# Last expert's row tiles one after the other with two scatters inside the branch, and the first gate's short tile scattered first

## The chip, the core and the metric

The program runs on one core of one Trainium2 chip. The metric is the device time of one execution in microseconds (us). Engines are named as in the profile: PE (matrix engine), PEld (its weight loads), DVE, ACT, POOL (GpSimd) and SP; a q behind a name (POOLq, SPq) is the engine's sequencer, which decodes, waits and branches while the engine itself may be idle or still busy. L1971 is line 1971 of the kernel before.

## What is computed

Attention with a decay over 4 batches of 576 tokens and 8 heads of 64 gives 2304 tokens of 512 numbers. A first mixture of 8 experts (512 to 1024 to 512, ReLU) sends each token to its best expert. A second mixture does the same with a hard capacity of 288 tokens per expert, assigned greedily by the largest logits. Cut to what matters here:

```python
def _moe_ref(x, w_gate, w_output_gate, w1, w2):
    logits = x @ w_gate
    e_idx = np.argmax(logits, axis=1)
    ...
        out[mask] = gate_w[mask, None] * eom[mask, e, None] * (np.maximum(x[mask] @ w1[e], 0.0) @ w2[e])
def _moe2_ref(x, w_gate, w1, w2):
    cap = N // E                       # 288
    ...                                # the largest logits take the places
    for e in range(E):
        mask = assigned == e
        out[mask] = np.maximum(x[mask] @ w1[e], 0.0) @ w2[e]
```

## The kernel before

The work goes through three stages on the same engines. Attention runs over 16 pairs of heads; `Router.gate` (L375 to L458) follows each batch: it makes logits, ranks each token inside its expert, and writes the rows of x to the DRAM array `xs` in expert order with five indirect scatters on POOL (L452), one for each 128-token tile. The fifth tile of a batch has only 64 real tokens, in partitions 64 to 127; the other 64 partitions get an index out of bounds (L442) and are dropped. After the fourth gate, `Moe1` fetches `xs` expert by expert, and its first weights and rows wait for the landing of the last scatter.

The second mixture is `Moe2Quick`. An expert has 288 rows: two tiles of 128 and a rest of 32. W1 runs column-wise for all 288 (L732). W2 runs by rows in `by_row` (L789): for each of 8 slices f of the hidden layer, three matmuls of 512 columns for tile 0 and three for tile 1 (L796), and the rest in two blocks of 16 small matmuls, `over(0)` after f = 3 and `over(4)` before f = 7 (L803). The three results are copied by ACT (L817 for the rest, L827 for the tiles) and scattered to the output on POOL (`send`, L1971). Each PE matmul of the tiles is one third of an fp32 product; an expert's W2 weights are all split (ACT L698, POOL L702) before its `by_row` ends.

For the first seven experts the scatters run during the next expert. The eighth writes to tiles `last` and `lastr`, which live outside the branch, and `finish` (L1977) scatters them at the very end of the program. Between the two lies control flow that every engine goes through:

```python
    with tc.If(uneven < 1):            # L2072, the normal case: both mixtures
        ...
            quick.go(redo, last)
    with tc.If(uneven > 0):            # L2080, not taken
        ...
    again = nc.values_load(redo[0:1, 0:1], min_val=0, max_val=1)    # L2088
    with tc.If(again > 0):             # L2089, not taken
        ...
    late["quick"].finish(tc, *last, out)
```

An engine that skips a body still does two things at its end: it waits until its own work and, on POOL, all DMAs that POOL has issued (DMASW0 to DMASW7, eight semaphores) have come in, and then it brings the semaphores to the values that the body would have left. On POOL that last step is INC_SWDGE_SEM. The order of instructions on each engine is the order in which the generators yield them; there is no scheduler that would move them.

Of the kernel before, what the change touches and what calls it, by code (L numbers as in the profile page):

```python
# [17 lines left out]
B, H, S, D = 4, 8, 576, 64  # L18
N = B * S
DM = H * D  # L20
E = 8
NP = H // 2
NQ = 4
SQ = NQ * 128
TL = S - SQ
# [289 lines left out]
class Router:  # L315
# [59 lines left out]
    def gate(self, b, ots, x, r):  # L375
        nc, p, ps = self.nc, self.p, self.att.ps_t
        us = p.tile([128, S], F32, name="us")
        for c0 in (0, S // 2):
# [4 lines left out]
            nc.scalar.copy(us[:, c0:c0 + S // 2], t[:, :S // 2])  # L383
# [48 lines left out]
        nc.scalar.activation(los, los, AF.Exp, scale=-1.0)  # L432
        pos = p.tile([128, NI, E], F32, name="pos")
        nc.vector.tensor_add(pos, po[:, :NI, :], ec(self.carry))
        nc.vector.tensor_add(self.carry, self.carry, po[:, NI, :])
        yield
        nc.vector.tensor_mul(pos, pos, ohb)
        sl = p.tile([128, NI], F32, name="sl")
        nc.vector.tensor_reduce(sl, pos, axis=AX.X, op=ALU.add)
        idx = p.tile([128, NI], I32, name="idx")  # L440
        nc.vector.tensor_copy(idx, sl)
        nc.vector.memset(idx[:T0, NQ:], E * RS)  # L442
        yield
        sm = p.tile([128, NI], F32, name="smx")
        nc.vector.tensor_reduce(sm, d, axis=AX.X, op=ALU.add)
# [4 lines left out]
        for i in range(NI):  # L450
            nc.gpsimd.memset(self.sp1, 0.0)
            st = nc.gpsimd.indirect_dma_start(  # L452
                out=self.xs[:, :], out_offset=bass.IndirectOffsetOnAxis(ap=idx[:, i:i + 1], axis=0),
                in_=x[:, i, :], in_offset=None, bounds_check=E * RS - 1, oob_is_err=False)
# [177 lines left out]
class FFN:  # L632
# [156 lines left out]
    def by_row(self, r, hs, rest, yr):  # L789
# [4 lines left out]
        if yr is None:  # L794
            yr = self.rp.tile([128, n, DM], F32, name="yr"), self.rp.tile([128, 128], F32, name="yl")
# [11 lines left out]

        for f in range(NF):
# [796 lines left out]
class Moe2Quick(Moe2):  # L1605
# [371 lines left out]
    def finish(self, tc, y, slots, out):  # L1977

        scat = []
        for t in range(3):  # L1980
            self.send(out, y, slots[:, t:t + 1], t, scat)
# [22 lines left out]
    def go(self, redo, last):  # L2004
# [12 lines left out]
        for ph in range(E):  # L2017
            self.cur = ph
            y = L.paced(f.run(ph, self.CAP, f.px if self.turning == ph else self.ready[ph][0],
                              last[0] if ph == E - 1 else None), 0.405, "gpso")  # L2020
# [12 lines left out]
def kernel(  # L2033
# [27 lines left out]
    with ExitStack() as c1:  # L2061
# [7 lines left out]
    last = ((lp.tile([128, 2, DM], F32, name="last"), lp.tile([128, 128], F32, name="lastr")),  # L2069
            lp.tile([128, 3], I32, name="slots"))  # L2070
# [9 lines left out]
    with tc.If(uneven > 0):  # L2080
# [5 lines left out]
        for t in last[0]:  # L2086
            nc.gpsimd.memset(t, 0.0)
# [49 lines left out]
```

## Time and profile before

| | |
|---|---|
| time, median of 3 runs | 764.57 us (764.44 to 764.62) |
| the profiled execution's own time | 764.5 us |
| its span in the trace | 762.8 us |
| PE busy | 689.9 us, 90% |
| POOL busy | 485.4 us, 64% |
| granted PE clock over the span | 0.957 |
| attention with its gates, to the landing of the last `xs` scatter | 0 to 222.6 us |
| second mixture's last expert, W2 by rows | 736.6 to 750.15 us |
| the last expert's three scatters on POOL | 750.9 to 754.4 us |
| end of the span | 762.8 us |

The profiled execution is 0.07 us under the median, so sums are made against 764.5 us. 1.7 us of it lie outside the span. The profile's page gives shares over the whole program; for this change only two stretches matter, the end of the last gate (205 to 223 us) and everything after 736 us, and these are read from the chain of waits, the timeline and the lists by source line, where the sequencers' own instructions show too.

### The profile page before, as it was taken

What the parts mean: (1) busy time and instruction counts of PE and PEld (TensorE: products, weight loads), DVE (VectorE), ACT (ScalarE), POOL (GpSimd) and SP (SyncE); (2) the same over time, 40 slices, a digit from 0 to 9 for tenths busy, and PEclk for the clock granted to TensorE, in tenths of its full rate; (3) what the DMA queues carried; (4) which work ended last, traced back from release to release, by engine and by line L of the source; (5) the groups of instructions that cost most, each with busy time, mean ns of one, the idle gap of its engine ahead of it and who ended that gap; (6) DMA issues with size and microseconds to landing.
All of it is one profiled execution on the core that took longest, in us unless ns stands there. A gap on an engine that the chain in (4) does not pass through costs nothing.

```text
span 762.8 us, 16050 instructions
## 1 busy us (share of the span) xinstructions
PE 689.9 (90%) x5691; PEld 571.0 (75%) x5691; DVE 367.7 (48%) x1419; ACT 382.5 (50%) x893; POOL 485.4 (64%) x504
## 2 busy tenths in 40 slices
PE   6999999999719999999999998289999999989993
PEld 3566555565419999999999998177978878888892
DVE  4776785977722132232322334756766666541020
ACT  5877776677216354555555651134535344354430
POOL 6566228172247776776776781259879778797761
PEclk9999999999959999999999999579999999999997
DMA  7588656130158362835826710348644726457201
GB/s 213 172 294 299 195 173 221 63 125 1 63 168 308 111 205 95 296 108 188 270 94 225 245 67 14 93 151 255 230 142 167 252 76 213 147 197 246 63 34 39
DMA packets 79524, 124.33 MB, mean 163 GB/s; under 512 B 11117, under 2 KB 43885, under 8 KB 79424
## 3 DMA queue, kind: packets, MB, share of 16 engines
q1 hardware_dynamic: 72944, 103.80, 41.2%
q0 software_dynamic: 6288, 18.97, 6.9%
q8 instruction: 49, 0.80, 0.5%
q14 instruction: 51, 0.42, 0.2%
q10 hardware_dynamic: 192, 0.34, 0.1%
HBM read 101.08 MB, written 22.71 MB: 162 GB/s over the span
## 4 chain that ended last, share of the span: by engine, by line
PE 54%; issue 5%; POOL 4%; DMA 3%; DVE 3%; POOLq 0%; ACT 0%; SPq 0%; DVEq 0%
PE ph L732 36%; PE ph L796 10%; POOL wl L702 3%; PE ph L803 2%; DMA xg<-x,idx 1%; PE tq L842 1%; PE sq L1783 1%; PE tq L1932 1%; PE tq L719 1%; DMA wraw<-in_moe_w_dram 1%; DMA xs<-x,idx 1%; PE tq L1036 1%; DVE cmp L1752 1%; PE gq L1892 0%; DVE xl L1939 0%
## 5 line engine op out<-in xcount | busy, mean ns | idle before, releaser
L702 POOL TENSOR_TENSOR wl<-wraw,wh 128x1024 fp32r<-128x1024 f32 x128 | 305.2, 2399 | 86.1 <-ACT wh L698 83.2
L732 PE MATMUL ph<-xh,wh 128*128 128x288 f32 (+6 forms) x512 | 160.6, 314 | 0.6 <-ACT xh L1945 0.6
L732 PE MATMUL ph<-xl,wh 128*128 128x288 f32 (+6 forms) x512 | 153.8, 300 | 1.1 <-DVE xl L1939 1.1
L698 ACT CAST wh<-wraw 128x1024 fp32r<-128x1024 f32 x128 | 132.1, 1050 | 43.7 <-DMA wraw<-in_moe_w_dram 30.6
L732 PE MATMUL ph<-xh,wl 128*128 128x288 f32 (+6 forms) x512 | 153.2, 299 | 0.0
L736 DVE SCALAR_TENSOR_TENSOR hl<-ph,hh 128x256 fp32r<-128x256 f32 (+6 forms) x128 | 56.1, 442 | 103.2 <-ACT hh L760 58.7
L174 ACT ACTIVATE z<-z,mx 128x128 f32<-128x128 f32 (+2 forms) x144 | 83.9, 583 | 36.5 <-DVE mx L177 36.0
L732 PEld LDWEIGHTS ph<-xh,wh 128*128 128x128 f32 x512 | 97.8, 191 | 4.8 <-issue 3.4
L760 ACT ACTIVATE hh<-ph 128x256 fp32r<-128x256 f32 (+6 forms) x128 | 51.4, 402 | 97.0 <-PE ph L732 93.5
L732 PEld LDWEIGHTS ph<-xl,wh 128*128 128x128 f32 x512 | 97.9, 191 | 2.1 <-DVE xl L1939 1.8
L732 PEld LDWEIGHTS ph<-xh,wl 128*128 128x128 f32 x512 | 97.6, 191 | 0.2 <-POOL wl L702 0.2
L177 DVE CUSTOM_DVE_ANT_0 z<-ps,cx 128x128 f32<-128x128 f32 (+2 forms) x144 | 68.5, 517 | 38.9 <-PE ps L188 22.5
L732 PE MATMUL ph<-hh,wh 128*128 128x288 f32 (+6 forms) x256 | 79.3, 310 | 0.0
L732 PE MATMUL ph<-hh,wl 128*128 128x288 f32 (+6 forms) x256 | 76.8, 300 | 0.9 <-POOL wl L702 0.8
L732 PE MATMUL ph<-hl,wh 128*128 128x288 f32 (+6 forms) x256 | 76.8, 300 | 0.0
L151 POOL TENSOR_SCALAR_AFFINE_SELECT cx<-cb 128x256 f32<-128x256 f32 (+1 forms) x64 | 44.3, 726 | 42.9 <-DMA cb<-c8d 19.9
L452 POOL DMA_INDIRECT xs<-x,idx x20 | 19.9, 994 | 62.0 <-DVE x L448 28.8
L796 PE MATMUL ph<-wh,hh 128*128 128x512 f32 x128 | 53.9, 421 | 0.0
L796 PE MATMUL ph<-wh,hl 128*128 128x512 f32 x128 | 50.5, 394 | 0.0
L796 PE MATMUL ph<-wl,hh 128*128 128x512 f32 x128 | 50.3, 393 | 0.0
L188 PE MATMUL ps<-kd,qd 64*128 64x128 f32 (+3 forms) x256 | 49.6, 488 | 0.1
L732 PEld LDWEIGHTS ph<-hh,wl 128*128 128x128 f32 x256 | 48.3, 189 | 1.4 <-POOL wl L702 1.4
(338 smaller groups left out, 1211.3 us busy)
## 6 DMA issues: line engine op xcount, KB each, us to landing
wraw<-in_moe_w_dram SPq DMA_DIRECT2D x128, 512.0 KB, 5.5
cb<-c8d SPq DMA_DIRECT2D x15, 576.0 KB, 6.0
xs<-zrow SPq DMA_DIRECT2D x8, 803.1 KB
xg<-xs SPq DMA_DIRECT2D x6, 771.0 KB, 9.0
kd<-in_k_dram SPq DMA_DIRECT2D x16, 288.0 KB, 6.3
qd<-in_q_dram SPq DMA_DIRECT2D x16, 288.0 KB, 3.9
vt<-in_v_dram SPq DMA_DIRECT2D x4, 1024.0 KB
x<-zrow SPq DMA_DIRECT2D x1, 1080.0 KB
```

The source lines that it names most:

```text
L151: nc.gpsimd.affine_select(cx[:, :, CB0[i]:CB0[i] + w], cb[:, :, :w], pattern=[[0, 2], [-1, w]], compare_op=ALU.is_ge, fill=-8e9, base=128 ...
L174: nc.scalar.activation(z, z, AF.Exp, bias=mx[:, c:c + 1], scale=-1.0, accum_out=sm[:, c:c + 1])
L177: nc.vector.tensor_tensor_reduce(out=z, in0=p, in1=cx, scale=-0.125, scalar=3e38, op0=ALU.add, op1=ALU.min, accum_out=mx[:, c:c + 1])
L188: nc.tensor.matmul(p[:, j, o:o + w], lhsT=qd[h, 128 * i:128 * i + 128], rhs=kd[h, :w], start=True, stop=True, skip_group_check=True)
L452: st = nc.gpsimd.indirect_dma_start(out=self.xs[:, :], out_offset=bass.IndirectOffsetOnAxis(ap=idx[:, i:i + 1], axis=0), in_=x[:, i, :], i ...
L698: nc.scalar.copy(wh, t)
L702: nc.gpsimd.tensor_sub(wl[:, q], t[:, q], wh.bitcast(F32)[:, q])
L732: mm = lambda o, w, m, st, sp: nc.tensor.matmul(o, lhsT=w, rhs=m, start=st, stop=sp)
L736: nc.vector.scalar_tensor_tensor(out=hl[:, :W], in0=p[:, :W], scalar=0.0, in1=hh.bitcast(F32)[:, :W], op0=ALU.max, op1=ALU.subtract)
L760: nc.scalar.activation(hh[:, :W], p[:, :W], AF.Relu)
L796: mm = lambda o, w, m, st, sp: nc.tensor.matmul(o, lhsT=w, rhs=m, start=st, stop=sp)
L803: nc.tensor.matmul(ps[n][32 * g:32 * g + 32, :128], lhsT=rest[f], rhs=self.raws[s][:, o:o + 128], start=f == 0, stop=f == NF - 1, skip_gro ...
```

## The change

In `by_row` the last expert gets a path of its own: `over(0)` and `over(4)` first, ACT copies the rest, POOL scatters it; then all 24 matmuls of tile 0, its copy and its scatter; then all 24 of tile 1, copied to `last`. The two scatters are issued on POOL inside the `If(uneven < 1)` body; `finish` keeps one scatter, of tile 1. In the gate the short tile gets an index tile of its own with 64 entries and is scattered first, without the dropped partitions; a sum is moved before the positions; the second half of the last gate's `us` goes through DVE and not ACT.

```diff
-            nc.scalar.copy(us[:, c0:c0 + S // 2], t[:, :S // 2])
+            self.att.evac(us[:, c0:c0 + S // 2], t[:, :S // 2], b == B - 1 and c0)
...
+        sm = p.tile([128, NI], F32, name="smx")
+        nc.vector.tensor_reduce(sm, d, axis=AX.X, op=ALU.add)
         pos = p.tile([128, NI, E], F32, name="pos")
         nc.vector.tensor_add(pos, po[:, :NI, :], ec(self.carry))
+        nc.vector.tensor_mul(pos, pos, ohb)
         nc.vector.tensor_add(self.carry, self.carry, po[:, NI, :])
         yield
-        nc.vector.tensor_mul(pos, pos, ohb)
         sl = p.tile([128, NI], F32, name="sl")
         nc.vector.tensor_reduce(sl, pos, axis=AX.X, op=ALU.add)
-        idx = p.tile([128, NI], I32, name="idx")
-        nc.vector.tensor_copy(idx, sl)
-        nc.vector.memset(idx[:T0, NQ:], E * RS)
-        yield
-        sm = p.tile([128, NI], F32, name="smx")
-        nc.vector.tensor_reduce(sm, d, axis=AX.X, op=ALU.add)
+        idt = p.tile([TL, 1], I32, name="idt")
+        nc.vector.tensor_copy(idt, sl[T0:, NQ:])
+        idx = p.tile([128, NQ], I32, name="idx")
+        nc.vector.tensor_copy(idx, sl[:, :NQ])
+        yield
...
-        for i in range(NI):
+        for ix, src in [(idt, x[T0:, NQ, :])] + [(idx[:, i:i + 1], x[:, i, :]) for i in range(NQ)]:
             nc.gpsimd.memset(self.sp1, 0.0)
             st = nc.gpsimd.indirect_dma_start(
...
+        if send:
+            for f0 in (0, 4):
+                over(f0)
+                yield 1.1
+            nc.scalar.copy(yr[1], ps[n][:, :128])
+            send(yr, 2)
+            for t in range(n):
+                w = slice(128 * t, 128 * t + 128)
+                for f in range(NF):
...
+                    mm(ps[t], hh[:, w], wh[:, m], f == 0, False)
+                    mm(ps[t], hh[:, w], wl[:, m], False, False)
+                    mm(ps[t], hl[:, w], wh[:, m], False, f == NF - 1)
+                    if f < NF - 1 or t < n - 1:
+                        yield 0.68
+                send(yr, t, ps[t])
+            return yr
...
-        scat = []
-        for t in range(3):
-            self.send(out, y, slots[:, t:t + 1], t, scat)
+        self.nc.gpsimd.indirect_dma_start(
+            out=out[:, :], out_offset=bass.IndirectOffsetOnAxis(ap=slot, axis=0), in_=y, in_offset=None,
+            bounds_check=N - 1, oob_is_err=False)
+
+    def part(self, idx, last, scat):
+
+        def send(y, t, p=None):
+            if t == 1:
+                self.nc.scalar.copy(last, p)
+                return
+            if t == 0:
+                self.nc.scalar.copy(y[0][:, 0, :], p)
+            self.nc.gpsimd.memset(self.sp1, 0.0)
+            self.send(self.o, y, idx[:, t + t // 2:t + t // 2 + 1], t, scat)
...
-        slots = last[1]
-        nc.vector.tensor_copy(slots[:, :2], idx[:, :2])
-        nc.vector.tensor_copy(slots[:, 2:], idx[:, 3:])
+        nc.vector.tensor_copy(last[1], idx[:, 1:2])
```

Three places show what moves. First POOL, from the last two weight splits (wl) to the branch that skips L2080. Before:

```order
L702 TENSOR_TENSOR wl<-wraw,wh 128x1024 [waits DMAHW0_49,PE_49,Activation_49]
L702 TENSOR_TENSOR wl<-wraw,wh 128x1024 [waits DMAHW1_49,PE_49,Activation_49]
L2072 UNCONDITIONAL_BRANCH
L2072 ISA [waits Pool_49,DMASW4_49,DMASW5_49,DMASW3_49,DMASW6_49,DMASW2_49,DMASW7_49,DMASW1_49,DMASW0_49]
L2072 UNCONDITIONAL_BRANCH
L2080 COMPARE_AND_BRANCH
```

and now, with the rest (yl) and tile 0 (yr) scattered there:

```order
L703 TENSOR_TENSOR wl<-wraw,wh 128x1024 [waits DMAHW0_49,PE_49,Activation_49]
L703 TENSOR_TENSOR wl<-wraw,wh 128x1024 [waits DMAHW1_49,PE_49,Activation_49]
L2010 MEMSET sp_433 1x1 [waits Pool_49]
L1991 DMA out_dram<-yl,idx_9509 9216x128 [waits DMASW5_49,DMASW6_49,DMASW0_49,DMASW7_49,DVE_49,Activation_49]
L2010 MEMSET sp_433 1x1 [waits Pool_49]
L1991 DMA out_dram<-yr,idx_9509 2304x512 [waits DMASW1_49,Activation_49]
L2101 UNCONDITIONAL_BRANCH
L2101 ISA [waits Pool_49,DMASW4_49,DMASW5_49,DMASW3_49,DMASW6_49,DMASW2_49,DMASW7_49,DMASW1_49,DMASW0_49]
L2101 UNCONDITIONAL_BRANCH
L2109 COMPARE_AND_BRANCH
```

Two scatters that wait for ACT now stand in POOL's queue ahead of both branches (L2080 and L2089 before, L2109 and L2117 now). Second, the end of POOL's skip of the first of these and what follows, now:

```order
L2109 ISA [waits Pool_49,Pool_sequencer_49,DMASW4_49,DMASW5_49,DMASW3_49,DMASW6_49,DMASW2_49,DMASW7_49,DMASW1_49,DMASW0_49]
L2109 UNCONDITIONAL_BRANCH
L2116 TENSOR_LOAD redo_3024 [waits DVE_49]
L2117 COMPARE_AND_BRANCH
```

These rows are the same in both kernels but for their line numbers; the ISA row waits for all eight semaphores of POOL's DMAs, and now the scatter of tile 0 is one of them. Third, DVE in the fourth gate, from the sum of the output gate's logits (los) to the scale that is written into x. The difference:

```order
 L431 TENSOR_REDUCE los<-lo_2931 128x5 [waits DVE_49]
-L434 TENSOR_TENSOR pos<-tp,carry 128x40 [waits PE_49]
-L435 TENSOR_TENSOR carry<-carry,tp 128x8 [waits DVE_49]
-L437 TENSOR_TENSOR pos<-pos,ohb 128x40
-L439 TENSOR_REDUCE sl<-pos 128x5 [waits DVE_49]
-L441 CAST idx<-sl 128x5 [waits DVE_49]
-L442 MEMSET idx 64x1 [waits DVE_49]
-L445 TENSOR_REDUCE smx<-d 128x5 [waits Activation_49]
+L434 TENSOR_REDUCE smx<-d 128x5 [waits Activation_49]
+L436 TENSOR_TENSOR pos<-tp,carry 128x40 [waits PE_49]
+L437 TENSOR_TENSOR pos<-pos,ohb 128x40 [waits DVE_49]
+L438 TENSOR_TENSOR carry<-carry,tp 128x8
```

The sum smx stands before pos and no longer after the index; the memset of the index is gone, and the cast is two casts.

## Rows read from the trace of the kernel before

**Rows 1.** The page's fourth part: the chain that ended last, by engine.

```profile
PE 54%; issue 5%; POOL 4%; DMA 3%; DVE 3%; POOLq 0%; ACT 0%; SPq 0%; DVEq 0%
```

**Rows 2.** Chain from 735 us: start us, us, what (xcount).

```profile
736.61 5.56 PE ph L796 x24
742.17 1.01 PE ph L803 x32
...
748.55 1.60 PE ph L796 x6
...
750.17 0.59 ACT last L827
...
753.45 0.97 POOL out_dram L1971
```

**Rows 3.** Source L2132 from 735 us: engine op xcount, ns min/median/max, first and last start us.

```profile
L2132 POOLq EVENT_SEMAPHORE  x4: 17/17/17, 762.0 to 762.7; - x4
L2132 POOLq DRAIN  x3: 46/113/10214, 751.7 to 762.5; - x3
L2132 SPq DRAIN  x3: 7/7/13, 757.9 to 762.2; - x3
L2132 PEldq DRAIN  x2: 8/8/8, 757.4 to 762.4; - x2
L2132 ACTq DRAIN  x2: 8/8/8, 757.8 to 762.2; - x2
```

**Rows 4.** Sources L2080, L2088, L2089 and L1971 from 735 us: POOL's sequencer, one row of DVE's.

```profile
L2080 POOLq EVENT_SEMAPHORE  x6: 17/30/43, 738.8 to 739.2; - x6
L2080 DVEq EVENT_SEMAPHORE  x2: 21/21/21, 742.1 to 742.2; - x2
...
L2080 POOLq INC_SWDGE_SEM  x1: 1948/1948/1948, 739.3 to 739.3; - x1
...
L2088 POOLq TENSOR_LOAD <-redo x1: 314/314/314, 742.2 to 742.2; - x1
...
L2089 POOLq COMPARE_BRANCH  x1: 58/58/58, 742.5 to 742.5; - x1
L2089 POOLq EVENT_SEMAPHORE  x5: 17/43/43, 745.4 to 745.8; - x5
...
L2089 POOLq INC_SWDGE_SEM  x1: 1917/1917/1917, 745.8 to 745.8; - x1
...
L1971 POOLq EVENT_SEMAPHORE  x7: 17/43/1322, 747.9 to 748.8; - x7
```

**Rows 5.** Timeline of POOL from 735 us: start us, us, engine line op, [idle before <-releaser].

```profile
750.88 0.99 POOL L1971 DMA_INDIRECT out_dram<-last,slots  x1 [12.13 <-ACT last L827]
752.17 0.97 POOL L1971 DMA_INDIRECT out_dram<-last,slots  x1 [0.30 <-issue]
```

**Rows 6.** DMA issues of the whole trace: engine op xcount, median us to landing.

```profile
x<-yr,idx POOLq DMA_INDIRECT x23, 2.8
out_dram<-yr,idx POOLq DMA_INDIRECT x14, 6.3
out_dram<-lastr,slots POOLq DMA_INDIRECT x1, 3.9
```

**Rows 7.** Timeline of DVE and POOL in the last gate.

```profile
209.98 0.20 DVE L431 TENSOR_REDUCE los<-lo 128x5 f32<-128x40 f32 x1
210.37 0.20 DVE L434 TENSOR_TENSOR pos<-tp,carry 128x40 f32<-128x40 f32 x1 [0.20 <-PE tp L421]
211.35 0.19 DVE L445 TENSOR_REDUCE smx<-d 128x5 f32<-128x40 f32 x1
211.58 0.17 DVE L446 TENSOR_SCALAR smx<-smx 128x5 f32<-128x5 f32 x1
212.05 0.19 DVE L448 RECIPROCAL x<-smx 128x5 f32<-128x5 f32 x1
212.52 0.98 POOL L452 DMA_INDIRECT xs<-x,idx  x1 [6.66 <-DVE key L466]
217.70 0.97 POOL L452 DMA_INDIRECT xs<-x,idx  x1 [0.23 <-issue]
```

**Rows 8.** Tile xs, landing of the fourth scatter, then of the fifth.

```profile
DMA to landing us min/median/max: 5.4/5.4/5.4
...
DMA to landing us min/median/max: 4.9/4.9/4.9
```

**Rows 9.** Source L1075: scatters of the first mixture, whole and partial tiles.

```profile
L1075 POOL DMA_INDIRECT x<-yr,idx x23: 892/967/1012, 271.2 to 475.9; - x23
```

**Rows 10.** Timeline of ACT in the last gate: the two halves of us.

```profile
204.50 0.88 ACT L383 COPY us<-tp 128x288 f32<-128x288 f32 x2 [2.66 <-PE tp L381]
```

**Rows 11.** DMA queues from 736.6 to 750.2 us: packets, MB, share of 16 engines.

```profile
DMA packets 12, 0.11 MB, mean 8 GB/s; under 512 B 0, under 2 KB 0, under 8 KB 0
...
q14 instruction: 10, 0.08, 1.6%
q8 instruction: 2, 0.03, 0.9%
```

More of the change, by code (lines that the diff above doesn't have):

```diff
@@ L449, in gate @@
         yield
-        for i in range(NI):
+        for ix, src in [(idt, x[T0:, NQ, :])] + [(idx[:, i:i + 1], x[:, i, :]) for i in range(NQ)]:
             nc.gpsimd.memset(self.sp1, 0.0)
             st = nc.gpsimd.indirect_dma_start(
-                out=self.xs[:, :], out_offset=bass.IndirectOffsetOnAxis(ap=idx[:, i:i + 1], axis=0),
-                in_=x[:, i, :], in_offset=None, bounds_check=E * RS - 1, oob_is_err=False)
+                out=self.xs[:, :], out_offset=bass.IndirectOffsetOnAxis(ap=ix, axis=0),
+                in_=src, in_offset=None, bounds_check=E * RS - 1, oob_is_err=False)
             for o in self.scat:
@@ L793, in by_row @@
         ps = [self.ps_h.tile([128, 512], F32, name="ph") for _ in range(n + 1)]
-        if yr is None:
-            yr = self.rp.tile([128, n, DM], F32, name="yr"), self.rp.tile([128, 128], F32, name="yl")
+        send = yr
+        yr = self.rp.tile([128, n, DM], F32, name="yr"), self.rp.tile([128, 128], F32, name="yl")
         mm = lambda o, w, m, st, sp: nc.tensor.matmul(o, lhsT=w, rhs=m, start=st, stop=sp)
@@ L806, in over @@
                     self.raws.pop(s)
+        if send:
[7 more added lines that the diff above has]
+                for f in range(NF):
+                    wh, wl = self.ws[8 * r + 4 + f // 2]
+                    hh, hl = hs[f]
+                    m = slice(512 * (f % 2), 512 * (f % 2) + 512)
+                    mm(ps[t], hh[:, w], wh[:, m], f == 0, False)
[5 more added lines that the diff above has]
+            return yr
         for f in range(NF):
@@ L1975, in send, with finish @@
         scat.append(st)
-    def finish(self, tc, y, slots, out):
-        scat = []
-        for t in range(3):
-            self.send(out, y, slots[:, t:t + 1], t, scat)
+    def finish(self, tc, y, slot, out):
+        self.nc.gpsimd.indirect_dma_start(
[10 more added lines that the diff above has]
+            self.send(self.o, y, idx[:, t + t // 2:t + t // 2 + 1], t, scat)
+        return send
     def settle(self, redo):
@@ L2018, in go @@
             self.cur = ph
-            y = L.paced(f.run(ph, self.CAP, f.px if self.turning == ph else self.ready[ph][0],
-                              last[0] if ph == E - 1 else None), 0.405, "gpso")
+            send = self.part(self.ready[ph][1], last[0], []) if ph == E - 1 else None
+            y = L.paced(f.run(ph, self.CAP, f.px if self.turning == ph else self.ready[ph][0], send), 0.405, "gpso")
             idx = self.ready.pop(ph)[1]
@@ L2068 @@
     lp = ctx.enter_context(tc.tile_pool(name="lp", bufs=1))
-    last = ((lp.tile([128, 2, DM], F32, name="last"), lp.tile([128, 128], F32, name="lastr")),
-            lp.tile([128, 3], I32, name="slots"))
+    last = lp.tile([128, DM], F32, name="last"), lp.tile([128, 1], I32, name="slot")
     uneven = nc.values_load(odd[0:1, 0:1], min_val=0, max_val=1)
@@ L2085 @@
         nc.vector.memset(redo, 1)
-        for t in last[0]:
-            nc.gpsimd.memset(t, 0.0)
+        nc.gpsimd.memset(last[0], 0.0)
     again = nc.values_load(redo[0:1, 0:1], min_val=0, max_val=1)
```

## The prediction

> **What bounds the kernel now.** I read the page's chain first, then the end of the program, then the last gate. The page puts 54% of the chain on PE and 4% on POOL [rows 1]: for most of the program PE sets the pace, and the change takes no matmul away. So only its ends matter. The chain from 735 us shows the last expert's W2 as one unbroken run on PE to 750.15 us, then ACT's copy of 0.59 us, then POOL's scatters, the last of which is issued by 753.45 + 0.97 = 754.42 us [rows 2, 5]. The span ends at 762.8 us, 8.4 us later, and the chain does not say why.
>
> The sequencers do. PE, ACT and SP are ready to stop at 757.4, 757.8 and 757.9 us [rows 3]. POOL's DRAIN starts at 751.7 and takes 10.2 us, to 761.9 us; only then does POOL release the others and everything stops 0.85 us later [rows 3]. **The end of the program is POOL's.** It is 761.9 - 754.4 = 7.5 us behind the end of POOL's last scatter.
>
> The second thing to see is what POOL does while PE computes the last W2. POOL has split its last weights by 738.8 us and then skips the two untaken branches [rows 4]: checks of its semaphores from 738.8, INC_SWDGE_SEM from 739.3 for 1.95 us, the load of `redo` at 742.2, the branch at 742.5, the first instruction behind it at 745.4, INC_SWDGE_SEM from 745.8 for 1.92 us, and the checks ahead of the final scatters, the seventh of which starts at 748.8 us. That is 10.0 us from 738.8 to 748.8, all beside PE, and only after it does POOL wait for ACT. The slack is 1.3 us: the seventh check takes 1.32 us, to 750.1 [rows 4].
>
> **The change, part by part.** *PE's order.* Both blocks of the rest go ahead of the tiles. No matmul is added. Tile 0 is done after two blocks of 1.01 us and 24 matmuls of 5.56 us together [rows 2]: 736.61 + 2.02 + 5.56 = 744.2 us. PE still ends at about 750.1 us.
>
> *Rest and tile 0 on POOL.* The rest's scatter is issued at some 739 us and costs POOL 1 us where it had nothing to do; free, since POOL next waits for tile 0. ACT's copy of tile 0 ends at 744.2 + 0.6 = 744.8 us [rows 2]; the scatter starts at 745.0 (0.1 to 0.6 us after, the first from the chain's gap between copy and scatter, the second an estimate for the checks ahead of it). What stands behind it in POOL's queue is both skips. The first of them waits for the landing of all of POOL's DMAs, tile 0's now among them.
>
> *Landing of tile 0.* The trace has no scatter to the output in a quiet stretch with nothing behind it. Nearest are x<-yr, of the same size, at 2.8 us, and the program's last one at 3.9 us; the far end is 6.3 us for the output's scatters beside the weight stream [rows 6]. From 736.6 to 750.2 us only 12 packets move, all of them instructions [rows 11], so I take 3.5 us, between the two near ones: 748.5 us. The branch ahead of the skip costs 2.9 us in its twin (742.5 to 745.4 [rows 4]) and runs beside the landing: 745.3 + 2.9 = 748.2 us, hidden by it.
>
> *The skips, now behind tile 0* [rows 4]. Checks 0.5 us (738.8 to 739.3): INC_SWDGE_SEM starts at 749.0 and ends at 750.95. The load of `redo`, 0.1 + 0.3 us, since the 0.9 us that stood before it (741.25 to 742.2) ended with DVE's own skip at 742.1 [rows 4], which is long done by then: 751.35. Branch 2.9 us: 754.25. Checks 0.4 us, INC_SWDGE_SEM 1.92 us: 756.6. Checks ahead of `finish`, 1.0 us: 757.6. The scatter starts 0.1 to 0.8 us behind its last check (the first scatter of before starts at 750.88, 0.8 us after 750.1); I take 0.4: 758.0, and it is issued by 759.0 us.
>
> *What is saved.* Two of the three final scatters leave the end: the third started 753.45 - 750.88 = 2.57 us after the first [rows 2, 5]. That is the gain, and it is in the numbers above: the last scatter is issued by 759.0 and not by 754.4 us, 4.6 us later in spite of it. Without the skips behind tile 0 it would have been issued by 751.9.
>
> *The tail.* Only one execution shows a DRAIN behind scatters, so what it waits for is bounded: if it ends 7.5 us behind the last scatter's issue [rows 3, 5], the span ends 4.6 us later. If it is counted from the last landing (753.45 + 3.9 = 757.35 us [rows 6], 4.55 us ahead of its end), the new landing at 758.0 + 2.8 to 3.9 puts it 3.5 to 4.6 us later. I take 4.55, since both readings meet there.
>
> *The gate.* Between los and pos DVE waits 0.2 us for PE [rows 7]. The sum smx, which took 0.23 us of the chain to the scale (211.35 to 211.58), fits in there but for 0.07 us; the memset leaves and one small cast comes, 0.1 us at most as an estimate from such rows. The reciprocal, at 212.05 before, and with it the five scatters [rows 7], come 0.2 us earlier. The last scatter now carries 128 real rows and not 64: its landing took 4.9 us, the full one before it 5.4 [rows 8]. So the landing on which the first mixture waits moves by -0.2 us to +0.3 us; I take -0.1, as the bytes in flight are the same in total. The Trainium skill's page "DMA: Bandwidth & Descriptors", in its fit per DMA, gives 2.0 us and the bytes over 436e3, which makes the full tile 0.3 us dearer than the half (an estimate from its figure); the trace's two landings do not contradict it, and by it the gate's term would be +0.1 and the sum 0.2 us more. The short tile's own issue, with 64 partitions, costs what partial and whole tiles cost in the first mixture, 0.89 to 1.01 us [rows 9]: nothing. The half of `us` on DVE frees ACT, whose two copies take 0.88 us together [rows 10], but the second can start only when PE has written it: 0, within 0.1 us either way.
>
> Sum: 4.55 - 0.1 = +4.45 us on the profiled execution's 764.5 us, which is 0.07 us under the median: **769.0 us**, slower by 0.6%. A measurement of this kernel can tell 0.2%, some 1.5 us, from no change.
>
> **Rivals.** *First, the drain grows with the scatters queued ahead of it.* This is the case on the other side. DRAIN starts before the second and the third scatter of before [rows 3, 5]; if its 7.5 us are 2.5 us for each of three, one scatter leaves 759.0 + 2.5 = 761.5 us, and the landing at 760.8 to 761.9 and the others' checks of 0.6 us come in at about the same time: the span ends near 762.5, the time is 764.1 us, not slower. It decides where the tail behind the last scatter falls under 7.5 - 4.6 = 2.9 us. For it: nothing in the trace shows what DRAIN does for 7.5 us. Against it: POOL goes on to other work within 0.3 us of each scatter wherever one is followed by something [rows 5].
>
> *Second, the drain takes a fixed time.* It starts 0.8 us after the first final scatter and lasts 10.2 us [rows 3, 5]: 758.0 + 0.8 + 10.2 + 0.85 gives 769.85 us of span, 7.05 us more: 771.5 us with the gate. The scatters that run behind its start speak against it. The Trainium skill's "Perfetto Trace Analysis", on sequencer-only instructions, says that the profile shows their execution and leaves their wait for a semaphore out; by that rule the 10.2 us would be DRAIN's own and the time would be this rival's, but no run here shows which.
>
> *Third, tile 0 lands late*, beside instruction fetches of the engines that branch at about that time (12 such packets before, [rows 11]): 6.3 us [rows 6] and not 3.5, 2.8 us more: 771.8 us.
>
> *Fourth, the change does not delay POOL as said:* the sequencer runs ahead and skips the first branch while the scatter is in flight. The ISA row that waits for all eight semaphores speaks against it, and even with no landing and no fetch to wait for, the path from 746.0 (the scatter's end) takes 0.5 + 1.95 + 0.4 + 2.9 + 0.4 + 1.92 + 1.0 + 0.4 = 9.5 us, to 755.5: 2.5 us less than the forecast, 766.5 us.
>
> **How the numbers follow.** Forecast with its bounds (766.6 to 770.7 us, from landing, start and tail at their ends): 0.57. Fourth rival, beside it: 0.05. Second: 0.10. Third: 0.06. First: 0.22, with times of 762.8 to 765.5 us. The range goes from 765.0 to 771.8 us: it leaves out most of the first rival and what is above the third. Faster by over 0.2% is under 763.0 us, the lower end of the first rival: 0.08. Within 0.2% is to 766.1 us, the rest of it and a little of the others: 0.16. Slower: 0.76.
>
> **What would show it.** Right: POOL's first INC_SWDGE_SEM near 749 us and not 739, after tile 0's landing; `redo` loaded on POOL near 751; one scatter of `last` near 758 us, and no wait for ACT ahead of it; DRAIN ending 7 to 8 us behind that scatter; PE, ACT and SP done by 758 us or waiting for that scatter. In the gate, the reciprocal near 211.85 us and the landing of the last scatter within 0.3 us of 222.6. What would make the prediction wrong: a final scatter before 754 us would say that POOL's skips are not held by tile 0, and a DRAIN that ends within 3 us of the scatter would be the first rival.

## The result, and the profile after

| | median us (range, runs) | ratio to before, 95% interval |
|---|---|---|
| before | 764.5 (762.04 to 766.06, 8) | |
| after | 769.24 (766.36 to 770.95, 8) | 1.0061 [1.0045, 1.0077] |

The change costs 4.7 us, 0.6%; the forecast was 769.0 us. The profiled execution of the changed kernel took 770.34 us, with a span of 768.5 us where before has 762.8, so the profiles differ by 5.8 us and not by 4.7. A part of that lies outside the tail, at the last gate, and is told at the end of this section.

**The end of the program.** The timeline of POOL from 735 us (start us, us, engine, line, what, idle before and its releaser) stands against [rows 5]:

```profile
740.15 0.99 POOL L1991 DMA_INDIRECT out_dram<-yl,idx  x1 [0.36 <-ACT yl L813]
741.13 0.09 POOL L2010 MEMSET sp<- 1x1 f32 x1
746.21 0.97 POOL L1991 DMA_INDIRECT out_dram<-yr,idx  x1 [4.99 <-ACT yr L2009]
759.21 0.97 POOL L1998 DMA_INDIRECT out_dram<-last,slot  x1 [12.03 <-issue]
```

The rest and tile 0 go out at 740.15 and 746.21 us, while PE still multiplies. The last scatter then stands idle for 12.03 us behind "issue": no engine released it, POOL's own sequencer did. In before, the same field names ACT, the copy of the last tile. ACT's copy is done early here too, as the timeline of ACT shows:

```profile
750.92 0.58 ACT L2006 COPY last<-ph 128x512 f32<-128x512 f32 x1 [4.99 <-PE ph L797]
```

So the rows are ready at 751.5 us and leave at 759.21. What POOL's sequencer does in the 7.7 us between shows in the rows of the two branches, of the load of `redo` and of `finish` (engine, operation, count, ns min/median/max, first and last start), which answer to [rows 4]:

```profile
L2109 POOLq EVENT_SEMAPHORE  x6: 17/30/542, 749.3 to 749.8; - x6
...
L2109 POOLq INC_SWDGE_SEM  x1: 1988/1988/1988, 750.4 to 750.4; - x1
```
```profile
L2116 POOLq TENSOR_LOAD <-redo x1: 313/313/313, 752.4 to 752.4; - x1
```
```profile
L2117 POOLq EVENT_SEMAPHORE  x5: 17/42/43, 755.4 to 755.7; - x5
...
L2117 POOLq COMPARE_BRANCH  x1: 58/58/58, 752.8 to 752.8; - x1
...
L2117 POOLq INC_SWDGE_SEM  x1: 1957/1957/1957, 755.8 to 755.8; - x1
```
```profile
L1998 POOLq EVENT_SEMAPHORE  x7: 17/43/43, 757.9 to 758.4; - x7
```

Every step of [rows 4] is there again, with its old length to within 0.3 us, 10 to 11 us later: the first INC_SWDGE_SEM starts at 750.4 and not at 739.3, the second at 755.8 and not at 745.8. The seventh check of `finish`, which took 1.32 us in before because it waited for ACT, takes 0.043 us: nothing is awaited any more. One check takes 0.54 us, the last of the six of line 2109, at 749.8; it ends at 750.3, when tile 0's rows have landed. The landing times of line 1991's two scatters:

```profile
DMA to landing us min/median/max: 2.4/3.2/4.1
```

The rest landed after 2.4 us, tile 0 after 4.1. Behind the last scatter comes the DRAIN of the program's end, which answers to [rows 3]:

```profile
L2160 POOLq DRAIN  x3: 46/113/8706, 759.0 to 768.3; - x3
L2160 SPq DRAIN  x3: 7/7/13, 762.6 to 768.0; - x3
...
L2160 PEldq DRAIN  x2: 8/8/8, 755.4 to 768.0; - x2
L2160 ACTq DRAIN  x2: 8/8/8, 757.1 to 768.0; - x2
```

It lasts 8.7 us where it lasted 10.2, but it ends at 767.7, again 7.5 us behind the end of the last scatter (759.21 + 0.97 = 760.18). All other engines are done by 762.6.

The last W1 matmul, before and then after (timeline of PE):

```profile
736.31 0.29 PE L732 MATMUL ph<-xh,wl 128*128 128x288 f32 x1
```
```profile
737.36 0.29 PE L733 MATMUL ph<-xh,wl 128*128 128x288 f32 x1
```

From its start to the end of the span it is 26.48 us before and 31.19 after: **the tail costs 4.7 us**, the whole of what the timed runs show.

**The last gate.** The rest of the profiles' difference, 1.05 us, is there when the last W1 begins. It arises at 204 us, where the gate's 16 matmuls of line 381 ran with a granted clock of 0.50, the lower of the two levels, instead of 1.00. The window 204.0 to 206.5 us of before, then this one and 206.5 to 209.0 us of after (busy us and count of PE, PEld, DVE, ACT and POOL, granted clock, DMA share, GB/s):

```profile
204.00:206.50 2.50, 1.90 (x21) 0.77 (x13) 0.60 (x2) 0.80 (x2) 1.62 (x5) 1.00 0.48 179
```
```profile
204.00:206.50 2.50, 2.50 (x19) 0.83 (x12) 0.55 (x2) 0.40 (x1) 1.18 (x4) 0.50 0.53 207
206.50:209.00 2.50, 0.79 (x3) 0.39 (x3) 1.82 (x3) 0.00 (x0) 0.00 (x0) 0.81 0.01 3
```

and line 381 in after, then in before (ns min/median/max):

```profile
L381 PE MATMUL tp<-ot,wgb x16: 530/684/685, 203.8 to 205.1; 128*32 128x288 f32 x16
```
```profile
L381 PE MATMUL tp<-ot,wgb x16: 406/406/430, 203.7 to 204.5; 128*32 128x288 f32 x16
```

From there all runs 0.9 to 1.2 us late. DVE's chain itself is shorter, as the timeline of DVE in after shows beside [rows 7]:

```profile
207.12 0.69 DVE L391 TENSOR_TENSOR g<-tp,r 128x512 f32<-128x512 f32 x1 [0.78 <-PE tp L389]
...
211.33 0.20 DVE L434 TENSOR_REDUCE smx<-d 128x5 f32<-128x40 f32 x1
211.59 0.20 DVE L436 TENSOR_TENSOR pos<-tp,carry 128x40 f32<-128x40 f32 x1
...
213.00 0.19 DVE L449 RECIPROCAL x<-smx 128x5 f32<-128x5 f32 x1
```

The sum `smx` fills the gap ahead of pos; from the start of g to that of the reciprocal it is 5.88 us, in before 6.14 (205.91 to 212.05). Whether the low clock belongs to the change was open at this point.

### The profile page after: what moved, and what is told of

Same layout as the page of the kernel before. It is cut to its first block, busy times and chain, and to the rows that moved or that the text cites. A ratio compares the mean times of both kernels' runs of the same rounds, so it can differ in the third digit from the quotient of the medians.

```text
span 768.5 us, 16058 instructions
## 1 busy us (share of the span) xinstructions
PE 689.3 (90%) x5691; PEld 571.4 (74%) x5691; DVE 368.9 (48%) x1419; ACT 382.0 (50%) x892; POOL 485.1 (63%) x506
## 4 chain that ended last, share of the span: by engine, by line
PE 48%; issue 7%; DMA 7%; POOL 6%; DVE 3%; POOLq 0%; SPq 0%; ACT 0%; DVEq 0%
PE ph L733 34%; PE ph L797 7%; POOL wl L703 5%; DMA out_dram<-yl,idx 3%; DMA xg<-x,idx 1%; PE tq L862 1%; PE tq L720 1%; PE ph L804 1%; PE sq L1803 1%; PE tq L1952 1%; DMA wraw<-in_moe_w_dram 1%; DMA xs<-x,idx 1%; PE tq L1056 1%; DMA xr<-x,idx 0%; PE gq L1912 0%
## 5 line engine op out<-in xcount | busy, mean ns | idle before, releaser
L216 PEld LDWEIGHTS tp<-ident,z 128*128 128x128 f32 x320 | 34.7, 141 | 20.0 <-issue 5.9
L216 PE MATMUL tp<-ident,z 128*128 128x128 f32 x320 | 45.9, 280 | 3.3 <-DVE carry L438 2.0
```

What stands on the lines that cost most here:

```text
L216: nc.tensor.transpose(o, z[:, CB0[i] + 128 * kb:CB0[i] + 128 * kb + 128], self.ident)
```

## The experiments

The theory: POOL leaves the branch later, and everything that its sequencer does on its way out (landing, two INC_SWDGE_SEM, a load, a branch, checks) then lies in a row ahead of the last scatter; behind it comes a tail of 7.5 us. Rivals: the gate part has a share (its low clock); DRAIN's time depends on the scatters just ahead of it or on their landing; the new order of the products costs time of itself. Since single runs of both kernels lie within some 5 us of one another, each reading rests on two things: the ratio of the timed runs, and one stretch of the profile, from the end of the last matmul to the end of the span (12.7 us before, 17.7 after).

**The two parts apart.** `gate_only` is before with this part of the change:

```diff
-            nc.scalar.copy(us[:, c0:c0 + S // 2], t[:, :S // 2])
+            self.att.evac(us[:, c0:c0 + S // 2], t[:, :S // 2], b == B - 1 and c0)
...
-        for i in range(NI):
+        for ix, src in [(idt, x[T0:, NQ, :])] + [(idx[:, i:i + 1], x[:, i, :]) for i in range(NQ)]:
```

> The kernel before with the change's gate part alone. The theory that the last expert's tail carries the whole loss and that the gate is worth nothing expects the time of the kernel before, from 0.2 us faster to 0.3 us slower, with the first xs scatter 0.2 us earlier to 0.1 us later against the first of the gate's matmuls of line 389. The rival, that the gate part itself made the 1.06 us which the changed kernel's profile shows at the last gate (granted TensorE clock 0.50 in 204 to 206.5 us, where the kernel before had 1.00), expects that low clock again here, the first xs scatter near 213.4 us instead of 212.5, and some 1.0 us more in all.

`tail_only` is before with the other part:

```diff
+            send(yr, 2)
...
+                send(yr, t, ps[t])
```

> The kernel before with the change's part at the last expert alone. The theory that the tail carries the loss expects, from the first W2 matmul of the last expert to the end of the span, 30.9 us as in the whole change (26.2 before), and 4.6 us more than before in the time. If the gate part made 1.06 us of the loss, this kernel is 1.06 us shorter than the whole change, with the clock at the last gate at 1.00 as before; if the low clock there has nothing to do with the gate part, it may show here too.

`gate_only` gave 0.9975 [0.9959, 0.9991], `tail_only` 1.0063 [1.0042, 1.0084], both beside the same runs of before (765.46 us). The tail alone carries the whole loss. The low clock is in neither profile: line 381 in `gate_only` has a median of 406 ns, and its first scatter to `xs` starts at 212.56 us, within 0.04 us of before. In `tail_only` the last matmul is 18.2 us ahead of the end, 0.6 more than in the whole change: tile 0 took 4.4 us to land there (0.3 more), and the first check behind the second branch came 2.9 us after it and not 2.6.

The gain of 0.25% in `gate_only` has no place in its profile, which ends 0.2 us later than that of before, and the pair further down denies it.

**What DRAIN waits for.** `all_inside` sends tile 1 inside the branch too, so that nothing stands behind the branches:

```diff
-            if t == 1:
-                self.nc.scalar.copy(last, p)
-                return
-            if t == 0:
-                self.nc.scalar.copy(y[0][:, 0, :], p)
+            if t < 2:
+                self.nc.scalar.copy(y[0][:, t, :], p)
...
-    late["quick"].finish(tc, *last, out)
```

> The whole change, but the second tile's rows are copied and scattered inside the branch like the first tile's, and nothing is left behind the two branches. The last scatter should then be issued by 752.5 us and land by 756.5, the first skip's INC_SWDGE_SEM runs to 758.5, the load and the branch to 761.6, the second skip to 763.6. Theory A, that the end waits 7.5 us from the last scatter's issue and that this time runs on while the skips run: 752.5 + 7.5 = 760.0 is over by then, and the span ends near 764, 4.5 us below the whole change and 2 us above before. Theory B, that the drain takes its 7.5 us from wherever it starts: it starts at 763.6 and the span ends near 771.5, 3 us above the whole change.

It gave 1.0079 [1.0048, 1.0110]. The last scatter and the DRAIN in its profile (timeline of POOL, then the rows of the branch and of the end):

```profile
749.25 0.97 POOL L1991 DMA_INDIRECT out_dram<-yr,idx  x1 [4.53 <-ACT yr L2006]
```
```profile
L2112 POOLq INC_SWDGE_SEM  x1: 1977/1977/1977, 759.2 to 759.2; - x1
```
```profile
L2153 POOLq DRAIN  x3: 46/107/7504, 761.2 to 769.2; - x3
```

Theory B: the last scatter is issued by 750.2 us and has landed at 753.5, the second skip ends at 761.1, and the DRAIN still takes 7.504 us from there. It waits here neither for an issue nor for a landing. It takes 7.5 us from the point at which POOL has nothing else left to do, one scatter or three ahead of it. From the last matmul to the end it is 21.2 us, 3.5 more than in the whole change; in the timed runs it is 1.4 us more, and their intervals do not tell the two kernels apart.

**One skip fewer.** `no_again` has no second branch:

```diff
-    again = nc.values_load(redo[0:1, 0:1], min_val=0, max_val=1)
-    with tc.If(again > 0):
-        with ExitStack() as c3:
-            m2.open(c3, m1.x2, moe2_w1, moe2_w2, out)
-            m2.go()
-        nc.gpsimd.memset(last[1], NK * N)
```

> The whole change without the second branch, so without the fallback that computes the second mixture again when the flag redo is set (on these inputs it is not). The theory that the last scatter waits for two skips in a row, each with its own INC_SWDGE_SEM and the second with a load and a branch of its own: the 5.4 us from the load (752.41) to the end of the second INC_SWDGE_SEM (757.79) are gone, the last scatter is issued from 753.8 instead of 759.2, and the span ends 5.4 us below the whole change, 7.5 us behind the last scatter as before. The rival, that the scatter behind the branches waits mostly for the landing of the first tile's rows (750.3) plus something fixed, expects less than 2 us.

0.9989 [0.9974, 1.0003], so at before's time and 0.7% below the whole change's ratio. From the last matmul to the end it is 13.2 us, 4.5 below after. The 5.4 us are gone; 0.6 came back with the landing of tile 0, which took 4.7 us in this run, and 0.3 between the DRAIN's end and the span's:

```profile
L2109 POOLq EVENT_SEMAPHORE  x6: 17/30/1673, 747.5 to 748.0; - x6
...
L2109 POOLq INC_SWDGE_SEM  x1: 1988/1988/1988, 749.7 to 749.7; - x1
```

The long check is the wait for the landing: 1.67 us, where after has 0.54. The skips in a row are the price, and the landing stands ahead of them.

**The order of the products without the scatters.** `three_behind` keeps the whole change but for the places of the scatters:

```diff
-            nc.scalar.copy(yr[1], ps[n][:, :128])
-            send(yr, 2)
+            nc.scalar.copy(send.rest, ps[n][:, :128])
...
+        for t in (2, 0, 1):
+            o = out[:, :] if t < 2 else out.rearrange("n (a c) -> (n a) c", c=128)
...
-            if t == 1:
-                self.nc.scalar.copy(last, p)
...
+            if t < 2:
+                self.nc.scalar.copy(last[t], p)
```

> The whole change, but all three scatters stand behind the two branches as before, in the order rest, first tile, second tile. Theory: the loss lies only in the scatters inside the branch, and not in the order of the W2 products. POOL has then passed both skips by the time of before (some 12.5 us behind the start of the last W1 stage), issues the rest and the first tile while TensorE finishes, and the second tile last: 1.28 us from one scatter to the next give the end of the last one 16.4 us behind the start of W1, where before has 18.1 and the whole change 22.8. So 1.7 us less than before (1.3 to 2.2) and 6.4 less than the whole change, with 7.5 us of drain behind it. The rival, that the order of the products itself costs time, expects the kernel before's time or more.

`three_plain` is its twin with the gate of before:

> The same as the kernel with three scatters behind the branches, with the gate of before instead of the gate part. If the gate part is worth nothing, the two differ by under 0.5 us and this one too is 1.7 us below before. If the gate part is worth the 0.25% (1.9 us) that its own run showed, this one is 1.9 us above its twin and equals before.

`three_behind` gave 0.9995 [0.9980, 1.0011], `three_plain` 0.9978 [0.9964, 0.9992], beside the same runs of before (764.08 us). Their last matmuls are 11.7 and 11.8 us ahead of the end, 0.8 to 1.0 us better than before; PE's W2 too is 0.3 us shorter in the new order (13.5 us from the last W1 to the last matmul instead of 13.8). That is 1.1 to 1.3 us of the 1.7 expected, at or just under the lower end of what was written. The order of the products costs nothing; by the profiles it gains about 1 us as long as no scatter stands in the branch, and the timed ratios of 0.9995 and 0.9978 do not contradict that. The gate part came out 0.17% the worse here and 0.25% the better in its own run: these contradict each other in sign, so **the gate part is worth nothing that these runs can tell**. They also show that two kernels can differ by 0.2% in these ratios without a cause in their profiles, although the intervals are narrower.

**One scatter in the branch.** `rest_inside` leaves only the rest's scatter there:

```diff
-            if t == 1:
-                self.nc.scalar.copy(last, p)
+            if t < 2:
+                self.nc.scalar.copy(last[t], p)
                 return
...
+        for t in (0, 1):
```

> The whole change, but only the rest's scatter stays inside the branch; the two tiles' scatters stand behind the branches. Theory: what costs is when POOL leaves the branch, and each step behind it follows in a row. The rest's scatter is issued 3.8 us behind the start of the last W1 stage and has landed 1.4 us later, the first skip's fetch and INC_SWDGE_SEM run to 9.3, load and branch to 12.4, the second INC_SWDGE_SEM to 14.8, the checks to 16.1, and the two scatters to 18.3, where before has 18.1 and the whole change 22.8: 0.2 us above before, 4.5 us below the whole change. The rival, that any scatter inside the branch costs the whole loss, since both INC_SWDGE_SEM then count it, expects 4 us or more above before.

1.0017 [1.0001, 1.0033]: 1.3 us above before in the timed runs, 0.2 expected. Its profile is worse than that, 15.7 us from the last matmul to the end, with the last scatter at 20.9 us behind the start of W1 instead of 18.3:

```profile
L2121 POOLq EVENT_SEMAPHORE  x5: 17/43/43, 752.0 to 754.4; - x5
L2121 POOLq INC_SWDGE_SEM  x1: 1937/1937/1937, 754.5 to 754.5; - x1
```

The first check behind its second branch comes 3.6 us after the branch (748.4 to 752.0), and between the five checks, which take 0.4 us in the other kernels, the sequencer stood still for another 2.1 us. One other kernel has both, `before_drains` below (3.6 and 2.4 us), and there no scatter stands in the branch; so this stall is not shown to be the scatter's. The way out of a branch is not of one length: the first check behind the second branch came 2.6 to 3.6 us after it in the profiles here. The Trainium skill's "Runtime: NRT & Kernel Launch", under instruction fetch mechanics, says that a taken branch to a page that is not at hand waits for that page to be fetched. It gives no time for that; the runs show a wait behind the branch, and not that it is for a page.

Ordered by what stands in the branch, the end comes 11.7 (nothing), 15.7 (the rest), 17.7 (rest and tile 0) and 21.2 us (all) behind the last matmul; 3.1 of the 15.7 us are the longer way out of `rest_inside` just told.

**Where DRAIN's time comes from.** `drain_early` is `three_behind` with one line more:

```diff
             quick.go(redo, last)
+        nc.gpsimd.drain()
```

> The kernel with three scatters behind the branches, and a DRAIN of POOL's own at the end of the first branch, behind the seventh expert's scatters. Theory A, that each DRAIN that follows scatters takes 7.5 us: it runs in POOL's idle time, but to 741.5 us, and so starts the skips 2.5 to 3 us later; the last scatter ends 3 us later than in its twin and the DRAIN at the end takes 7.5 us again, so 3 us above the twin. Theory B, that the 7.5 us come once, for all that POOL did since the start of the program: the DRAIN at the end is short (some 0.1 us, as the second and third ones there are), the end then waits for the last landing, and the time is 1 to 4 us below the twin.

1.0031 [1.0014, 1.0048], 0.36% above its twin and so near the 3 us of theory A, but neither theory holds as a whole. POOL's last work ahead of the new DRAIN (timeline), then the rows of the new DRAIN, of the first skip and of the end:

```profile
733.38 4.74 POOL L703 TENSOR_TENSOR wl<-wraw,wh 128x1024 fp32r<-128x1024 f32 x2
```
```profile
L2112 POOLq DRAIN  x1: 11123/11123/11123, 734.3 to 734.3; - x1
```
```profile
L2113 POOLq INC_SWDGE_SEM  x1: 189/189/189, 749.3 to 749.3; - x1
```
```profile
L2165 POOLq DRAIN  x3: 46/113/4615, 757.6 to 763.3; - x3
```

The first DRAIN delays the skips, as theory A has it. Its row of 11.1 us starts while two weight splits are still at work; from their end (738.12) to its own (745.41) it is 7.3 us. But then INC_SWDGE_SEM takes 0.19 us and not 1.95, and the DRAIN at the end stops at 762.26, only 1.9 us behind the end of the last scatter (760.33) and 0.2 us behind the last landing in the trace (762.08): there the end waits for the landing, as theory B has it. So the two lengths go with what POOL has issued **since the last DRAIN**: 88 indirect transfers had gone by before the first, three before the second.

Two more kernels follow this up, on `three_plain`. `drain_mid` has one DRAIN where POOL was idle, ahead of the second mixture:

```diff
             self.xgs.append((x[:, 0, :], x[:, 1, :], xr))
+        self.nc.gpsimd.drain()
```

> The kernel with three scatters behind the branches and the gate of before (its twin), with one DRAIN of POOL's at the start of the second mixture, where POOL was idle for 13 us (479.3 to 492.4). The earlier run with a DRAIN in front of the branches left a DRAIN of 1.9 us behind the last scatter at the end and two INC_SWDGE_SEM of 0.2 us. Theory P, that a DRAIN works off what all indirect transfers since the last DRAIN left behind, and INC_SWDGE_SEM some of it too: here 48 of 91 indirect transfers follow the DRAIN, so the end keeps about half of its 7.5 us, 3 to 5 us, and the time is 2 to 4 us below the twin. Theory Q, that the length hangs on whether a DRAIN ran at all: 1.9 us at the end and the time 5 to 7 us below the twin. Theory R, that only a DRAIN behind the last regular scatters helps: 7.5 us and the twin's time.

`drain_many` has seven more:

```diff
         yield self.f.pace.t + 1.5
         scat = []
+        self.nc.gpsimd.drain()
```

> The same with one more DRAIN in front of each expert's three scatters in the second mixture (seven). Theory P: each works off six indirect transfers, 2 to 2.5 us, on POOL, which idles some 7 of an expert's 27 us; only the last expert's gathers and the seventh's scatters are left for the end, which takes 1.9 to 2.5 us instead of 7.5, and each INC_SWDGE_SEM 0.2 instead of 1.95, so POOL stands ready before TensorE ends: 5.6 us from the DRAIN, up to 1.7 from the scatters, less what POOL's later weight splits cost TensorE (0 to 5 us): 2 to 7 us below the twin. Theory Q expects the same 5 to 7 us as one DRAIN gives, less that loss.

They gave 0.9933 [0.9911, 0.9955] and 0.9857 [0.9833, 0.9882], beside runs of before that took 778.08 us in that session. Theory P: in `drain_mid` DRAIN ends 4.5 us behind the last scatter (765.14 to 769.68), in `drain_many` 3.5 us (760.20 to 763.65). The 3.5 us are more than P's 1.9 to 2.5, since the last landing in the trace came at 763.37 and DRAIN ended 0.3 us behind it. Their rows of INC_SWDGE_SEM in the first skip, `drain_mid` and then `drain_many2` (the same kernel as `drain_many`, below):

```profile
L2112 POOLq INC_SWDGE_SEM  x1: 1088/1088/1088, 751.7 to 751.7; - x1
```
```profile
L2113 POOLq INC_SWDGE_SEM  x1: 248/248/248, 741.5 to 741.5; - x1
```

A DRAIN that stands earlier shows what one costs by itself. The row of `drain_mid`'s DRAIN and, from the timeline, POOL's last work inside it; then both for the last DRAIN in `drain_many2`'s loop:

```profile
L2035 POOLq DRAIN  x1: 7565/7565/7565, 477.0 to 477.0; - x1
```
```profile
480.73 0.25 POOL L2033 MEMSET xr<- 128x128 f32 x1
```
```profile
L1981 POOLq DRAIN  x1: 2757/2757/2757, 726.6 to 726.6; - x1
```
```profile
726.68 2.41 POOL L702 TENSOR_TENSOR wl<-wraw,wh 128x1024 fp32r<-128x1024 f32 x1 [3.27 <-ACT wh L698]
```

Both rows hold a wait for work that was queued ahead. From the end of that work, the first takes 3.6 us (480.98 to 484.59) after 43 indirect transfers and the second 0.3 us (729.09 to 729.40) after three. With the 7.3 us after 88 in `drain_early` and the 7.5 us after 91 at the end of before, that is some 0.08 us for each transfer since the last DRAIN.

Because 1.4% was more than their ends could hold, the last two runs repeat `drain_many` beside before with the same eight DRAINs (`before_drains`):

> The kernel before with the eight DRAINs alone (one at the start of the second mixture, seven in front of an expert's scatters), its tail as it was. If the DRAINs pay at the end, whatever the order of the tail: the end stands some 8.6 us behind the last matmul instead of 12.6 (the DRAIN ends 3.5 us behind the last scatter instead of 7.5), so 4 us below before, 0.5% of the time; more if what the kernel with eight DRAINs gained on the chip of its run (1.4%) came in the loop over the experts too. If they pay only together with the new order of the last products, under 1 us.

> The kernel with eight DRAINs and three scatters behind the branches once more, beside its counterpart that has the tail of before, to tell how much of its 1.4% was the chip of that run. From the profiles at the end alone (7.6 us from the last matmul to the end, 12.6 before): 5 us, 0.65%, and 0.7 to 1.7 us below the counterpart. If the 1.4% is the kernel's, 0.9857 again within 0.3%.

`before_drains` gave 0.9985 [0.9969, 1.0000], `drain_many2` 0.9969 [0.9953, 0.9985], with before at 764.37 us. The ends are as expected, 8.8 and 7.6 us behind the last matmul.

But from the first W1 matmul of the second mixture to the last it is 240.6 and 237.5 us, where before has 237.2 and `three_plain` 236.4. In `before_drains` the loop so gives back 3.4 of the 3.8 us gained at the end, in `drain_many2` 1.1 of 4.2. What holds PE up is shown in part: its waits for the gathers of `xg`, which POOL issues, are 2.6 and 1.9 us long there, and 0.9 and 1.0 in before and `three_plain`; no wait of PE for POOL's weight splits shows. The loop alone also varies: it takes 234.9 us in `three_behind`, whose code there is that of `three_plain`. The 1.4% was not the kernel's alone; what more there was in that session, where the same loop took 247.0 and 242.5 us in `drain_mid` and `drain_many`, stays open.

The end of `before_drains`, its DRAIN and the landing of its last scatter, which starts at 758.81:

```profile
L2134 POOLq DRAIN  x3: 52/113/5151, 757.1 to 763.1; - x3
```
```profile
DMA to landing us min/median/max: 3.1/3.1/3.1
```

The landing comes at 761.95 and DRAIN ends at 762.24: after six transfers it is the landing that sets its end.

In `drain_many2` POOL is no longer last at the end:

```profile
L2165 POOLq DRAIN  x3: 52/112/4808, 751.7 to 758.4; - x3
...
L2165 PEldq DRAIN  x2: 8/8/8, 756.0 to 758.1; - x2
L2165 ACTq DRAIN  x2: 8/8/8, 757.8 to 758.1; - x2
```

POOL's DRAIN ends at 756.5 and ACT comes at 757.8, from its own way through the two branches behind its last copy. Outside the session of 778 us, the lowest ratio is `drain_many2`'s, 2.4 us under before; `three_plain`, 1.7 us under before, has an interval that overlaps with it and is the simpler of the two. Both intervals lie below before's time, where the changed kernel's ratio is 1.0061. Against before, ratios of this size are weak evidence, as the gate part's 0.25% shows; the ends in the profiles, 7.6 and 11.8 us behind the last matmul where before has 12.7, are what speaks for them.

## Why the prediction was right

- *The end is POOL's, and the skips go behind tile 0.* Held in each step. INC_SWDGE_SEM was put at 749.0, the load at 751, the second INC_SWDGE_SEM's end at 756.6 and the last scatter at 758.0; they came at 750.4, 752.4, 757.8 and 759.2, with the last W1 1.05 us late from the gate. From the start of the last W1 the scatter was issued 22.7 us on in the forecast (736.31 to 759.0) and 22.8 us in the run.
- *The terms of that sum* were each off, in part against one another; that they came to within 0.2 us is in part luck. Tile 0's copy ended at 745.93, its scatter began at 746.21; less the 1.05 us of the late start that is 745.16, where 745.0 stood. The landing took 4.1 us and not 3.5 (4.1 to 4.7 in four runs), but all checks except the last ran beside it, so INC_SWDGE_SEM started 0.07 us behind it and not 0.5. The second branch took 2.6 us to the first check and not 2.9, the checks of `finish` 0.6 and not 1.0, and the scatter started 0.77 us behind the last of them, not 0.4.
- *The tail.* 7.5 us behind the last scatter, as taken, but for neither of the two reasons weighed. The reading that counts from the last landing falls: in `all_inside` that landing was 7.7 us past when the DRAIN began. The reading that counts from the issue is right here only because the scatter is POOL's last work; `all_inside` shows that the DRAIN takes its 7.5 us from the end of whatever POOL does last. The term stayed the same because both kernels issue the same 91 indirect transfers and no DRAIN among them, which the prediction did not know.
- *The first rival* (2.5 us for each of three scatters) fell: one scatter left the same 7.5 us as three. Its mechanism was half right. The DRAIN does grow with the scatters, but with all indirect transfers since the last DRAIN and not with the last ones, and by some 0.08 us for each, not 2.5: 0.3 us after 3, 3.6 after 43, 7.5 after 91.
- *The second rival* (10.2 us from DRAIN's start) fell with its number, since the DRAIN lasted 8.7 us; its thought that the time is DRAIN's own, and no wait for data, held in both kernels; with only three or six transfers to work off, DRAIN did end with the last landing. The rule cited there, of the Trainium skill's "Perfetto Trace Analysis" on sequencer-only instructions, would have the whole row be execution. The trace disagrees where POOL has work queued: the row begins ahead of the last scatter (759.0 against 759.21) and contains that scatter's issue.
- *The third and fourth rivals* (a landing of 6.3 us, a skip that runs ahead) did not come: 4.1 us, and a check that waited for the landing.
- *The gate.* DVE's chain became 0.26 us shorter, as reckoned (0.2). The last scatter to `xs` landed 5.0 us behind its start (218.67 to 223.65), in before 4.9 [rows 8], within the bounds. Its sum of nothing stands in the timed runs, but the reciprocal and the scatters did not come 0.2 us earlier: in `gate_only`, with the clock as in before, the first scatter starts at 212.56 and not at 212.52 us. The prediction left out what takes the gain back. PE's idle time ahead of the matmuls of line 381 is 1.57 to 1.59 us in all seven profiles with the gate part and 1.30 in all seven without, because a copy on DVE ahead of them (line 275) takes 0.44 to 0.46 us and not 0.17; why it does is not shown. That the clock would fall at line 381 was not foreseen either. It did in two of the seven profiles with the gate part (`after`, and `rest_inside` in part: 500 ns at the median) and in none of the seven without. The longer idle time alone does not bring it, since the other five have it and kept the full clock. That the gate part makes this fall more likely is possible and not shown; the timed pairs show no cost.
- *What was wrong in the profile's own sum*: the 770.34 us of the profiled execution against 769.0 is the clock at the gate, 1.05 us, and the rest the errors above.

## What to carry to other kernels

Work that moves inside a branch delays all that its engine's sequencer does on the way out: here POOL's landing, checks, INC_SWDGE_SEM, load and branch, 12 us that but for the landing had been free beside PE, now stood ahead of the last scatter. Count these rows ahead of such a move, and issue the late work behind the branches instead. A DRAIN at the end of a program can cost several us where many indirect transfers were issued, here 7.5 us after 91; one that is run earlier, where POOL is idle, takes part of it off the end, and after that the last landing or the next late engine sets the end. What such a DRAIN costs where it stands must be counted too: in the loop here the eight took 1.1 to 3.4 us back.

## What the runs showed of the hardware

INC_SWDGE_SEM on POOL takes 0.19 us and 0.020 us more for each indirect transfer since the last DRAIN: 189 ns after none, 248 after 3, 1088 after 45, 1948 after 88 and 1988 after 90 (first skip of `drain_early`, `drain_many2`, `drain_mid`, before and after).

POOL's first DRAIN behind indirect transfers must be counted from the end of POOL's queued work, which its row contains: 0.31 us after 3 transfers, 0.56 after 6 (`drain_many2`'s loop), 3.61 after 43, 7.29 after 88 and 7.51 after 91, with or without an INC_SWDGE_SEM between. It did not end ahead of the last landing: at the end of the four programs with only 3 or 6 transfers since the DRAIN before, it came 0.2 to 0.3 us behind it. One row fits neither, 4.5 us after 48 at the end of `drain_mid`, where 0.08 us for each would give 4.0. The following DRAINs take 0.05 to 0.11 us. The Trainium skill's "VectorE: DVE Perf Modes", in its note on the two things called DRAIN, gives those that the runtime puts around a kernel as about 12 ns on every engine: 7 to 17 ns is what the other four engines show here, and POOL's 8706 ns is not of that size.
